# Attention and a gated feed-forward interleaved on one core: where the lead splits w_down, when keys are asked for, and the order of the handover and of the last output groups

## The chip, the cores and the metric

The kernel runs on one core of a Trainium2 chip. The metric is the device time of one execution in microseconds (us). Three runs of the kernel before took 2699.92 to 2701.48, with a median of 2700.95. One more execution was profiled; its own time was 2699.41, and its span from the first to the last instruction 2697.6.

## The reference

The input x is 2048 tokens of 576 numbers, all in 32-bit floats. There are 32 heads of 18, and the feed-forward is 4608 wide.

```python
def _A_ref(x, wqkv, wo):
    qkv = (x @ wqkv).reshape(B, S, 3, H, Dh).transpose(2, 0, 3, 1, 4)
    scores = jnp.einsum("bhqd,bhkd->bhqk", q, k) * (Dh ** -0.5)
    o = jnp.einsum("bhqk,bhkd->bhqd", _softmax(scores), v)
    return o.transpose(0, 2, 1, 3).reshape(B, S, D) @ wo

def _B_ref(x, w_gate, w_up, w_down):
    return (_gelu(x @ w_gate) * (x @ w_up)) @ w_down

xn = _layernorm(x)
return x + _A_ref(xn, ...) * _silu(_B_ref(xn, ...))
```

## The kernel before

**Numbers as two parts.** TensorE multiplies a reduced format. Each operand is therefore split into a high part and the rest (`hi`, `lo`), and each product is three matmuls: high with high, low with high, high with low. A split is two instructions: a copy that rounds (hi), and a subtraction (lo). `split` (L90) puts both on POOL. `split_av` (L95) puts the copy on ACT and the subtraction on DVE.

**Stages.** A prologue normalises x, projects queries, keys and values, and leaves them in DRAM. After it everything is cut into 144 sections of the feed-forward, made by `section` (L394). One section is a block of 512 tokens with 128 of the 4608 columns: 54 matmuls for gate (`pg`) and up (`pu`), then the gelu (`activate`, L357: t1 and t2 by turns on ACT and DVE). `finish` (L426) splits the section's result into `hh` and `hl`. Two sections share one piece of w_down (256 rows). Each odd section asks for it (`raw`), and its `finish` splits it into `dh` and `dl`. `downs` (L422) then runs the down projection of the pair, half after each of the next two sections: 24 matmuls into `py`, each group of six added to Y by DVE. The weights of the next section are asked for and split (`wh`, `wl`, always on POOL) while the present one runs.

- **Lead**: sections 0 to 8. Beside the feed-forward they hold the first score maxima. `FIRST` says how many slots each has (0, 3, 5, 5, 5, 5, 5, 6, 6); a slot is two matmuls `pm` and two maxima `mx` on DVE. Keys are loaded in chunks of eight slots by `load_k`, 12 DMAs each; a loop after each section decides which chunk to ask for (L702). `finish()` uses `split`, so hh, hl, dh and dl are on POOL.
- **Attention**: sections 9 to 136, by a loop over `n` from 0 to 127, with exponentials `pT` (ACT), values `acc` and maxima for a later unit.
- **Tail**: sections 137 to 143, `n` from 128 to 134, in the loop at L743. Here `finish` uses `split_av`. The attention's output of the last 512 tokens is loaded to `OT` (`load_o`, with `den` the reciprocal sums), multiplied (`norm_o`), split on POOL (`split_o`: `oh`, `ol`) and projected by `project_o`: eight groups of 15 matmuls `po`, each copied to `S2` by ACT. The groups are handed out by `at(n, part, ...)`: groups 0 to 3 in sections 138 to 141, groups 4 and 5 in 142, groups 6 and 7 in 143. After the last `downs` (48 matmuls) come, for each of the eight output pieces: tanh on ACT (L354), two DVE operations (L355, L762), the addition of x on POOL (L763) and a store.

**What sets the order.** Instructions of TensorE stand in the order written. A scheduler orders the other engines' instructions, but for those under `keep_in_program_order`. Every DMA goes through the one queue of SP, in order: a DMA that waits holds back those behind it. Each engine works its own queue in order too.

**Buffers.** The tag `raw` has two tiles in the pool `wts` (L99). Weights of gate and up and the raw w_down take turns in them; in sections 139 and later w_down has its own in the pool `epi`. `pT` has four tiles in the pool `att` and is first used by section 9. `wh` and `wl` have five, `hh` and `hl` three, `dh` and `dl` one until the tail and two there, t1 and t2 one, `oh` and `ol` one. In PSUM, `py` has two and `pm` and `po` three.

Of the kernel before, what the change touches and what calls it, by code (L numbers as in the profile page):

```python
# [8 lines left out]
F32 = mybir.dt.float32  # L9
# [57 lines left out]
def kernel(ctx: ExitStack, tc: tile.TileContext, x, wqkv, wo, w_gate, w_up, w_down, out):  # L67
# [22 lines left out]
    def split(hi, lo, raw):  # L90
        first = nc.gpsimd.tensor_scalar(hi, raw, 1.0, 1.0, op0=ALU.mult, op1=ALU.mult)  # L91
        nc.gpsimd.tensor_tensor(lo, raw, f(hi), op=ALU.subtract)  # L92
        return first

    def split_av(hi, lo, raw, keep=lambda i: i):  # L95
        keep(nc.scalar.activation(hi, raw, AF.Copy))  # L96
# [329 lines left out]
    def finish(pool=ffn, cut=split, bufs=1):  # L426

        n = FF["n"] - 1
        b, r = divmod(n // G, NR)
        hh = ffn.tile([P, TB], F32R, name="hh", bufs=G + 1)  # L430
        hl = ffn.tile([P, TB], F32R, name="hl", bufs=G + 1)
        cut(hh, hl, FF["act"])
        FF["hs"].append((hh, hl))
        if n % G == G - 1:
            wd = [pool.tile([P, G, D], F32R, name=m, bufs=bufs) for m in ("dh", "dl")]
            cut(*wd, FF["rawd"])
            for h in range(2):
                FF["down"].append((b, r, FF["hs"], wd, FF["Y"], (2 * h, 2 * h + 1), n + 1 + h))

# [29 lines left out]
    def split_o(i):  # L469

        j = i % (TB // P)
        oh, ol = (op.tile([KO, NK, P], F32R, name=m) for m in ("oh", "ol"))
        split(oh, ol, OT[:, :, j * P:(j + 1) * P])
        OG["o"] = oh, ol

# [14 lines left out]
        rows, cc = place(b, i)  # L490
        nc.sync.dma_start(out[rows, cc], OG.pop(("y", b, i)))

    def project_o(b, i, S2=None):
# [5 lines left out]
        o = OG["o"]  # L499
        terms = [(k, x, w) for k in range(NK) for x, w in ((0, 0), (0, 1), (1, 0))]  # L500
        for m, (k, x, w) in enumerate(terms):
            n = min(KO, D - k * KO)
            nc.tensor.matmul(po[:, 0:288], o[x][0:n, k, :], OW[w][0:n, k, :], start=(m == 0), stop=(m == len(terms) - 1))  # L503
        if b < NB - 1:
            nc.vector.scalar_tensor_tensor(yy, yy, 0.5, po[:, 0:288], op0=ALU.mult, op1=ALU.mult)
            nc.gpsimd.tensor_tensor(yy, yy, xx, op=ALU.add)
            OG["y", b, i] = yy
        else:
            nc.scalar.activation(S2[:, j, cc], po[:, 0:288], AF.Copy)

# [15 lines left out]
    for b in range(NB):  # L526
        last = b == NB - 1
        for k in range(NK):
            t0 = b * AB + max(-(-min(H, (k + 1) * HO) // QD) * NA + 3, 2 * NA + 10 + 3 * k)
            if not (last and k == NK - 1):  # L530
                at(t0, 0, load_o, b, k)
                at(t0 + 2 - last, 2, norm_o, k)
        first = (b + 1) * AB + 1 if last else max((b + 1) * AB + 6, (b + 1) * NR * G - len(FIRST) + 3)
        at(first - 2, 0, load_wo, 0)
        at(first - 1, 2, split_o, 0)
        for i in range(GROUPS):
            n = first + i
            past = i - (ENDS - 2 - first) if last else -1
            if past >= 0:
                n = ENDS - 2 + past // 2  # L540
            if not last:
                at(n, 0, load_xy, b, i)
                at(n + 1, 0, store_y, b, i)
            part = 3 if past >= 0 and past % 2 else 1
            at(n, part, lambda b=b, i=i: project_o(b, i, S2[0]))
            if i == TB // P - 1:
                at(n + 1, 0, load_wo, 1)
            if i + 1 < GROUPS:
                at(n, part + 1, split_o, i + 1)


    with tc.tile_pool(name="att", bufs=1, reuse_waits="tile") as att:
# [138 lines left out]
        def reciprocals(u, rt):  # L691
            den = DEN.pop(u)
            tc.keep_in_program_order(nc.vector.reciprocal(den, den))
            nc.sync.dma_start(rt.rearrange("a (c s) -> a c s", s=QD * TB // P), den)

        load_k(0)
        load_q(0)
        slot, chunk = 0, 1
        for n, m in enumerate(FIRST):
            section([lambda s=s: lead_pair(s) for s in range(slot, slot + m)], "s" if n == 1 else "f")  # L700
            slot += m
            while chunk < KB and chunk * SLOTS <= slot + 14:  # L702
                load_k(chunk, tc.keep_in_program_order)
                chunk += 1
            if n == 3:
# [31 lines left out]
    with tc.tile_pool(name="epi", bufs=1, reuse_waits="tile") as epi:  # L737
        S2[0] = epi.tile([P, TB // P, D], F32, name="S2")
        XX = epi.tile([P, TB // P, D], F32, name="XX")
        n = NU * NA  # L740
        load_o(NB - 1, NK - 1, epi)
        todo[n, 2].insert(0, lambda: norm_o(NK - 1))
        while FF["n"] < NF:  # L743
            section([], "m" if n % 2 else "f", wts if n < NU * NA + 2 else epi)
# [5 lines left out]
            for part in (2, 3, 4):  # L750
                tasks(n, part)
            finish(epi, lambda *t: split_av(*t, tc.keep_in_program_order), 2)
            n += 1
        assert not todo
        downs()
        for Y, j, c in finals:
            cc = slice(288 * c, 288 * c + 288)
            rows = slice(S - TB + j * P, S - TB + (j + 1) * P)
# [3 lines left out]
            nc.vector.scalar_tensor_tensor(ss, th, 0.5, ss, op0=ALU.mult, op1=ALU.mult)  # L762
            nc.gpsimd.tensor_tensor(ss, ss, XX[:, j, cc], op=ALU.add)  # L763
            nc.sync.dma_start(out[rows, cc], ss)


# [26 lines left out]
```

## Time and profile before

| what | us |
|---|---|
| median of three runs | 2700.95 |
| the profiled execution, its own time | 2699.41 |
| its span | 2697.6 |
| PE busy in it | 2654.8 |
| lead, first matmul of section 0 to the first of section 9 | 199.7 to 309.4 |
| attention, to the first matmul of section 137 | 309.4 to 2580.7 |
| tail | 2580.7 to 2697.6 |

The profile's views used below: a table of stretches gives for each its length and the busy time of each engine (and in brackets the number of instructions), then the clock that TensorE was granted as a share of full speed, and the DMA share and rate. The timeline gives an instruction's start, its duration, what it is (out<-in), and in square brackets how long the engine had been idle before it and which instruction or DMA ended that. The chain of waits gives the work that ended last, step by step. Some matmul records are missing, so counts can fall short by a few.

### The profile page before, as it was taken

The page shows a single profiled execution, that of the slowest core. Times are in us where ns is not written, and L with a number is a line of the kernel's source. Part 1 is how long each engine was busy: PE and PEld are TensorE (multiplying, and loading weights), DVE is VectorE, ACT ScalarE, POOL GpSimd, SP SyncE. Part 2 cuts the span into 40 slices and gives each one's busy share as a digit, 9 for nine tenths or more (in the row PEclk, how much of TensorE's full clock was granted, in tenths as well). Part 3 has the DMA queues.
Part 4 walks back from the last instruction along what each step waited for, and adds up shares of the span by engine and source line. Part 5 has one row for each costly group of instructions (what it writes and reads, how often), then busy time and mean ns, then how long its engine had stood idle before and what let it go on. Part 6 is the DMA issues. An engine that isn't in the chain of part 4 may idle for free.

```text
span 2697.6 us, 55502 instructions
## 1 busy us (share of the span) xinstructions
PE 2654.8 (98%) x21000; PEld 2041.0 (76%) x21000; DVE 2005.5 (74%) x3430; ACT 1430.2 (53%) x2542; POOL 1363.9 (51%) x1454
## 2 busy tenths in 40 slices
PE   8998999999999999999999999999999999999997
PEld 7887777777777777777777777777777777777676
DVE  6326888888888877788888877888888877888344
ACT  3221355556665555566656554566555555665622
POOL 2116644444465555545456555454456555444563
PEclk9999999999999999999999999999999999999999
DMA  8874433333354334533345344433435445333341
GB/s 256 262 235 125 111 95 102 104 104 103 101 141 116 102 102 119 137 104 103 103 111 147 102 115 128 130 102 99 103 98 138 118 121 140 104 100 87 75 117 39
DMA packets 389144, 323.65 MB, mean 120 GB/s; under 512 B 105544, under 2 KB 302664, under 8 KB 388876
## 3 DMA queue, kind: packets, MB, share of 16 engines
q1 hardware_dynamic: 388876, 320.08, 43.9%
q8 instruction: 167, 2.74, 0.4%
q14 instruction: 101, 0.83, 0.1%
HBM read 266.58 MB, written 52.85 MB: 118 GB/s over the span
## 4 chain that ended last, share of the span: by engine, by line
PE 94%; DVE 3%; POOL 2%; DMA 1%; ACT 1%; issue 0%; SPq 0%; POOLq 0%; DVEq 0%
PE pg L347 27%; PE acc L666 17%; PE py L377 17%; PE pe L632 10%; PE pm L605 9%; PE po L152 7%; PE pu L347 6%; PE po L503 2%; PE pt L206 0%; DMA raw<-in_B_w_up_dram 0%; DVE Y L355 0%; POOL wl L92 0%; DVE mx L606 0%; DVE Y L383 0%; POOL dl L92 0%
## 5 line engine op out<-in xcount | busy, mean ns | idle before, releaser
L633 ACT ACTIVATE pT<-pe 128x512 f32<-128x512 f32 x2048 | 1164.6, 598 | 770.5 <-PE pm L605 551.8
L606 DVE TENSOR_REDUCE mx<-pm 128x1 f32<-128x512 f32 x2048 | 1291.4, 685 | 57.6 <-PE pm L605 35.2
L347 PE MATMUL pg<-xd,wh 64*128 64x512 f32 x2592 | 949.9, 399 | 7.6 <-POOL wh L91 7.6
L347 PE MATMUL pu<-xd,wh 64*128 64x512 f32 x2592 | 950.5, 399 | 0.1
L632 PE MATMUL pe<-q,KS 56*128 56x512 f32 x2048 | 815.3, 406 | 0.1
L605 PE MATMUL pm<-KS,q 54*128 54x512 f32 x2048 | 798.0, 394 | 3.5 <-DVE mx L606 3.0
L91 POOL TENSOR_SCALAR wh<-raw 128x384 fp32r<-128x384 f32 x432 | 221.7, 514 | 888.0 <-DMA raw<-in_B_w_up_dram 505.3
L347 PEld LDWEIGHTS pg<-xd,wh 64*128 64x128 f32 x2592 | 484.5, 187 | 63.5 <-issue 21.1
L347 PE MATMUL pg<-xd,wl 64*128 64x512 f32 x1296 | 510.4, 394 | 1.3 <-POOL wl L92 1.3
L347 PE MATMUL pu<-xd,wl 64*128 64x512 f32 x1296 | 509.0, 393 | 0.0
L347 PEld LDWEIGHTS pu<-xd,wh 64*128 64x128 f32 x2592 | 485.8, 187 | 6.7 <-DVE t L364 1.3
L666 PE MATMUL acc<-pT,VS 128*32 128x512 f32 x4096 | 466.0, 595 | 0.0
L92 POOL TENSOR_TENSOR wl<-raw,wh 128x384 fp32r<-128x384 f32 x432 | 438.1, 1015 | 34.2
L632 PEld LDWEIGHTS pe<-q,KS 56*128 56x128 f32 x2048 | 369.0, 184 | 81.0 <-ACT pT L633 23.0
L383 DVE TENSOR_TENSOR Y<-py,Y 128x288 f32<-128x288 f32 x544 | 248.0, 457 | 207.4 <-PE py L377 206.7
L605 PEld LDWEIGHTS pm<-KS,q 54*128 54x128 f32 x2048 | 376.9, 185 | 33.1 <-DVE mx L606 7.5
L377 PE MATMUL py<-dh,hh 128*128 128x288 f32 x1152 | 358.0, 311 | 4.7 <-ACT dh L96 2.1
L377 PE MATMUL py<-dl,hh 128*128 128x288 f32 x1152 | 340.5, 296 | 3.7 <-POOL dl L92 2.7
L377 PE MATMUL py<-dh,hl 128*128 128x288 f32 x1152 | 339.0, 294 | 0.4 <-POOL hl L92 0.4
L666 PEld LDWEIGHTS acc<-pT,VS 128*32 128x32 f32 x4096 | 120.1, 109 | 276.6 <-issue 265.2
L377 PEld LDWEIGHTS py<-dh,hh 128*128 128x128 f32 x1152 | 216.6, 188 | 82.8 <-issue 44.6
L347 PEld LDWEIGHTS pg<-xd,wl 64*128 64x128 f32 x1296 | 243.1, 188 | 21.4 <-POOL wl L92 2.3
(104 smaller groups left out, 2816.1 us busy)
## 6 DMA issues: line engine op xcount, KB each, us to landing
KS<-qk SPq DMA_DIRECT2D x1536, 36.0 KB
raw<-in_B_w_gate_dram SPq DMA_DIRECT2D x144, 288.0 KB
raw<-in_B_w_up_dram SPq DMA_DIRECT2D x144, 288.0 KB
raw<-in_B_w_down_dram SPq DMA_DIRECT2D x72, 576.0 KB
VS<-vs SPq DMA_DIRECT2D x128, 152.0 KB
qk<-t SPq DMA_DIRECT2D x72, 256.0 KB
q<-qk SPq DMA_DIRECT2D x384, 36.0 KB
xd<-xhs SPq DMA_DIRECT2D x24, 384.0 KB
```

The costliest lines, as they stand in the source:

```text
L91: first = nc.gpsimd.tensor_scalar(hi, raw, 1.0, 1.0, op0=ALU.mult, op1=ALU.mult)
L92: nc.gpsimd.tensor_tensor(lo, raw, f(hi), op=ALU.subtract)
L152: nc.tensor.matmul(o, st, m, start=(i == 0), stop=(i == len(TERMS) - 1))
L347: nc.tensor.matmul(o, w[1 + wp][k][rr, c, :], xd[xp][k][rr, c, :], start=(i == 0), stop=(i == len(terms) - 1))
L377: nc.tensor.matmul(py, a[:, tt], w[:, g, cc], start=(n == 0), stop=(n == 3 * G - 1))
L383: nc.vector.tensor_tensor(yy, py, yy, op=ALU.add)
L503: nc.tensor.matmul(po[:, 0:288], o[x][0:n, k, :], OW[w][0:n, k, :], start=(m == 0), stop=(m == len(terms) - 1))
L605: nc.tensor.matmul(pm, QS[u, r][rr, t * P:(t + 1) * P], KS[(u * NA + c) % KB][r][rr, :], start=True, stop=True)
L606: nc.vector.tensor_reduce(MX[u][:, 2 * r + a, t, c:c + 1], pm, axis=AX.X, op=ALU.max)
L632: nc.tensor.matmul(pe, KS[(u * NA + c) % KB][r][rr, t * P:(t + 1) * P], QS[u, r][rr, :], start=True, stop=True)
L633: nc.scalar.activation(PT[u, kt][:, 2 * r + a, :], pe, AF.Exp, scale=SCALE)
L666: nc.tensor.matmul(ACC[u][32 * a:32 * a + 32, :], VS[(u * NA + c) % VB][:, v:v + 32], pt[:, a, :], start=(kt == 0), stop=(kt == NT - 1), s ...
```

## The change

Six edits are made.

1. In the lead, the raw w_down goes to a tile of `pT` in place of a `raw` tile (`lead_raw`).
2. In the lead, `finish` uses the new `split_ap`: the copies `hh` and `dh` on ACT, the subtractions `hl` and `dl` on POOL.
3. The test for the next chunk of keys has 11 in place of 14, so chunks 2, 4, 5 and 6 are asked for one section later.
4. At the handover, the last `load_o` stands after section 137's requests in place of before them, and the section whose DMAs and weight requests keep program order is 138 in place of 137 (`keep` in `section`). The scheduler then puts section 138's gate, up and w_down requests on SP before the store of the last `acc`.
5. In section 143 the last w_down is split early (`early`), at the start of the section.
6. Group 5 of `project_o` goes from section 142 to after section 143's `downs`; groups 6 and 7 go behind the last 48 matmuls. Their `oh` and `ol` are split ahead, group 7's into tiles of its own. These two groups aren't copied to S2: DVE multiplies the gate with `po` straight from PSUM, and DVE adds x. The other six pieces end as before.

```diff
+    def split_ap(hi, lo, raw):
+        nc.scalar.activation(hi, raw, AF.Copy)
+        nc.gpsimd.tensor_tensor(lo, raw, f(hi), op=ALU.subtract)
...
-    def section(specials=(), tag="f", pool=wts):
+    def section(specials=(), tag="f", raw_d=None, early=None):
...
-        keep = tc.keep_in_program_order if n == NU * NA + len(FIRST) else lambda i: i
+        keep = tc.keep_in_program_order if n == NU * NA + len(FIRST) + 1 else lambda i: i
...
-            raw = FF["rawd"] = raw_tile([P, G, D], pool)
+            raw = FF["rawd"] = raw_d() if raw_d else raw_tile([P, G, D])
             nc.sync.dma_start(raw, w_down[r * G * P:(r + 1) * G * P, :].rearrange("(g p) n -> p g n", p=P))
+            if early:
+                FF["wd"] = early(raw)
...
-            wd = [pool.tile([P, G, D], F32R, name=m, bufs=bufs) for m in ("dh", "dl")]
-            cut(*wd, FF["rawd"])
+            wd = FF.pop("wd", None)
+            if not wd:
+                wd = [pool.tile([P, G, D], F32R, name=m, bufs=bufs) for m in ("dh", "dl")]
+                cut(*wd, FF["rawd"])
...
+            if last and n >= ENDS - 1:
+                continue
...
-            part = 3 if past >= 0 and past % 2 else 1
-            at(n, part, lambda b=b, i=i: project_o(b, i, S2[0]))
+            at(n, 1, lambda b=b, i=i: project_o(b, i, S2[0]))
...
+        def lead_raw():
+            t = att.tile([P, QD, TB], F32, name="pT", bufs=4)
+            return t.rearrange("p a t -> p (a t)")[:, 0:G * D].rearrange("p (g d) -> p g d", g=G)
...
-            section([lambda s=s: lead_pair(s) for s in range(slot, slot + m)], "s" if n == 1 else "f")
+            section([lambda s=s: lead_pair(s) for s in range(slot, slot + m)], "s" if n == 1 else "f", lead_raw)
             slot += m
-            while chunk < KB and chunk * SLOTS <= slot + 14:
+            while chunk < KB and chunk * SLOTS <= slot + 11:
...
-            finish()
+            finish(cut=split_ap)
...
-        load_o(NB - 1, NK - 1, epi)
...
+            if n == NU * NA:
+                load_o(NB - 1, NK - 1, epi)
...
+        HIND = ENDS - 1 - (NU * NA + 1)
+        project_o(NB - 1, HIND, S2[0])
+        os = []
+        for i in range(HIND + 1, GROUPS):
+            split_o(i, op if i == HIND + 1 else epi)
+            os.append(OG.pop("o"))
         downs()
...
+            if c * (TB // P) + j > HIND:
+                late[c * (TB // P) + j] = th, ss, j, cc
+            else:
+                nc.vector.scalar_tensor_tensor(ss, th, 0.5, ss, op0=ALU.mult, op1=ALU.mult)
+                put(ss, j, cc, nc.gpsimd)
+        for i, o in zip(range(HIND + 1, GROUPS), os):
+            th, ss, j, cc = late[i]
+            po = project_o(NB - 1, i, o=o)
+            nc.vector.scalar_tensor_tensor(ss, th, 0.5, po, op0=ALU.mult, op1=ALU.mult)
+            put(ss, j, cc, nc.vector)
```

The number of matmuls is the same. In the attention's sections the order of instructions on every engine is the same as before.

More of the change, by code (lines that the diff above doesn't have):

```diff
@@ L467, in load_wo, with split_o @@
             nc.sync.dma_start(f(w)[0:D - m, NK - 1, :], wos[i, m:D, cc])
-    def split_o(i):
+    def split_o(i, pool=op):
         j = i % (TB // P)
-        oh, ol = (op.tile([KO, NK, P], F32R, name=m) for m in ("oh", "ol"))
+        oh, ol = (pool.tile([KO, NK, P], F32R, name=m) for m in ("oh", "ol"))
         split(oh, ol, OT[:, :, j * P:(j + 1) * P])
@@ L507, in project_o @@
             OG["y", b, i] = yy
-        else:
+        elif S2 is not None:
             nc.scalar.activation(S2[:, j, cc], po[:, 0:288], AF.Copy)
+        return po[:, 0:288]
     AB = NQ * NA
@@ L537 @@
             n = first + i
-            past = i - (ENDS - 2 - first) if last else -1
-            if past >= 0:
-                n = ENDS - 2 + past // 2
+            if last and n >= ENDS - 1:
+                continue
             if not last:
@@ L548 @@
             if i + 1 < GROUPS:
-                at(n, part + 1, split_o, i + 1)
+                at(n, 2, split_o, i + 1)
     with tc.tile_pool(name="att", bufs=1, reuse_waits="tile") as att:
@@ L740, with cut, early @@
         n = NU * NA
-        load_o(NB - 1, NK - 1, epi)
         todo[n, 2].insert(0, lambda: norm_o(NK - 1))
+        def cut(hi, lo, raw):
+            split_av(hi, lo, raw, tc.keep_in_program_order)
+        def early(raw):
+            wd = [epi.tile([P, G, D], F32R, name=m, bufs=2) for m in ("dh", "dl")]
+            cut(*wd, raw)
+            return wd
         while FF["n"] < NF:
-            section([], "m" if n % 2 else "f", wts if n < NU * NA + 2 else epi)
+            section([], "m" if n % 2 else "f", (lambda: raw_tile([P, G, D], epi)) if n > NU * NA + 1 else None,
+                    early if n == ENDS - 1 else None)
+            if n == NU * NA:
+                load_o(NB - 1, NK - 1, epi)
             if n == NU * NA + 3:
@@ L749, with put @@
             downs()
-            for part in (2, 3, 4):
-                tasks(n, part)
-            finish(epi, lambda *t: split_av(*t, tc.keep_in_program_order), 2)
+            tasks(n, 2)
+            finish(epi, cut, 2)
             n += 1
         assert not todo
-        downs()
+        HIND = ENDS - 1 - (NU * NA + 1)
[4 more added lines that the diff above has]
+            os.append(OG.pop("o"))
+        downs()
+        def put(ss, j, cc, add):
+            rows = slice(S - TB + j * P, S - TB + (j + 1) * P)
+            add.tensor_tensor(ss, ss, XX[:, j, cc], op=ALU.add)
+            nc.sync.dma_start(out[rows, cc], ss)
+        late = {}
         for Y, j, c in finals:
             cc = slice(288 * c, 288 * c + 288)
-            rows = slice(S - TB + j * P, S - TB + (j + 1) * P)
             th = epi.tile([P, 288], F32, name="thl", bufs=len(finals))
```

7 lines of the change are left out of this document (2 added, 5 removed).

## The prediction

> **What bounds the kernel now.** I read the page first, with the chain of waits.
>
> ```profile
> PE 2654.8 (98%) x21000; PEld 2041.0 (76%) x21000; DVE 2005.5 (74%) x3430; ACT 1430.2 (53%) x2542; POOL 1363.9 (51%) x1454
> PE 94%; DVE 3%; POOL 2%; DMA 1%; ACT 1%; issue 0%; SPq 0%; POOLq 0%; DVEq 0%
> ```
>
> TensorE (PE) sets the end nearly everywhere. The change takes no matmul away, so it can only win time in which PE stands, runs at a lower clock, or has finished. The chain names POOL, DMA and DVE for a few per cent, so I asked for stretches cut at the first `pg` matmul of each section. The lead from the end of section 2 on: its `py` work with the wait behind it, then one section a row from section 3 (section 4 is left out; its `py` part stands alone below), and two attention sections:
>
> ```profile
> 223.83:231.49 7.66, 3.73 (x26) 3.29 (x25) 4.39 (x9) 1.18 (x2) 3.65 (x5) 0.98 0.40 98
> 231.49:246.56 15.07, 14.14 (x89) 11.12 (x89) 9.12 (x16) 1.23 (x2) 8.19 (x11) 0.79 0.32 99
> ...
> 258.34:270.12 11.78, 11.66 (x90) 9.38 (x89) 9.85 (x18) 1.23 (x2) 6.30 (x8) 1.00 0.57 147
> 270.12:283.81 13.69, 12.18 (x89) 9.46 (x89) 9.93 (x18) 1.23 (x2) 10.07 (x10) 1.00 0.35 81
> 283.81:296.54 12.73, 12.49 (x94) 9.87 (x93) 11.61 (x23) 1.23 (x2) 6.39 (x8) 1.00 0.59 155
> 296.54:309.44 12.90, 11.64 (x92) 10.38 (x91) 10.47 (x19) 1.23 (x2) 10.06 (x10) 1.00 0.52 143
> 309.44:327.28 17.84, 17.77 (x144) 13.69 (x143) 14.24 (x24) 10.18 (x18) 8.88 (x12) 1.00 0.39 102
> 327.28:344.60 17.32, 17.32 (x143) 12.75 (x142) 14.00 (x23) 10.22 (x18) 11.72 (x13) 1.00 0.39 103
> ```
>
> ```profile
> 254.57:258.34 3.77, 3.65 (x26) 3.25 (x25) 3.64 (x8) 1.18 (x2) 2.16 (x3) 1.00 0.45 82
> ```
>
> An undisturbed lead section of five slots takes 11.78 with PE busy for 11.66. Section 3 takes 15.07, at a mean clock of 0.79, and section 6 takes 13.69. What they wait for stands in the timelines of PE, POOL, ACT and SP:
>
> ```profile
> 231.49 0.79 PE L347 MATMUL pg<-xd,wh 64*128 64x512 f32 x1 [3.02 <-POOL wh L91]
> ```
>
> ```profile
> 222.44 2.64 POOL L92 TENSOR_TENSOR dl<-raw,dh 128x1152 fp32r<-128x1152 f32 x1
> 229.00 0.62 POOL L91 TENSOR_SCALAR hh<-t 128x512 fp32r<-128x512 f32 x1 [3.92 <-DVE t L364]
> ...
> 246.72 1.15 POOL L91 TENSOR_SCALAR dh<-raw 128x1152 fp32r<-128x1152 f32 x1 [6.87 <-PE py L377]
> ...
> 271.50 0.51 POOL L91 TENSOR_SCALAR wh<-raw 128x384 fp32r<-128x384 f32 x1 [6.24 <-DMA raw<-in_B_w_up_dram]
> ```
>
> ```profile
> 215.24 0.60 ACT L360 ACTIVATE t<-pg 128x512 f32<-128x512 f32 x1 [6.58 <-POOL hl L92]
> ```
>
> ```profile
> 214.49 5.69 SPq L573 DMA_DIRECT2D KS<-qk  x12
> 220.28 0.62 SPq L106 DMA_DIRECT2D raw<-in_B_w_gate_dram  x1
> ```
>
> POOL is half idle, but in order: section 3's `wh` stands behind the `hh` at 229.00, which waits for DVE. Later it starves too: the weights at 271.50 are late, because w_down takes turns with them in the two `raw` tiles. The tail, cut the same way (section 143 with parts of its own):
>
> ```profile
> 2590.83:2594.86 4.03, 0.00 (x1) 0.00 (x0) 1.73 (x3) 0.89 (x2) 3.86 (x5) 0.79 1.07 304
> 2594.86:2609.92 15.06, 14.25 (x94) 11.91 (x94) 4.95 (x7) 3.18 (x5) 9.53 (x12) 0.83 0.52 126
> 2609.92:2622.08 12.16, 11.98 (x94) 10.43 (x93) 5.13 (x8) 2.07 (x4) 11.58 (x14) 1.00 0.66 195
> ...
> 2646.41:2660.55 14.14, 13.96 (x109) 12.41 (x108) 6.13 (x10) 2.91 (x5) 3.88 (x4) 1.00 0.14 50
> 2660.55:2676.82 16.27, 14.02 (x110) 12.47 (x109) 6.38 (x10) 4.55 (x8) 4.57 (x4) 1.00 0.00 1
> ...
> 2687.52:2697.60 10.08, 0.00 (x0) 0.00 (x0) 5.55 (x11) 0.44 (x1) 4.53 (x5) 0.56 0.25 89
> ```
>
> ```profile
> 2660.55:2666.94 6.39, 6.39 (x56) 5.30 (x55) 1.95 (x1) 0.93 (x2) 2.29 (x2) 1.00 0.00 0
> 2666.94:2669.02 2.08, 2.08 (x18) 2.08 (x17) 0.70 (x2) 1.23 (x2) 0.00 (x0) 1.00 0.00 0
> ...
> 2674.75:2676.82 2.07, 0.00 (x1) 0.01 (x1) 0.72 (x2) 1.98 (x3) 0.00 (x0) 1.00 0.00 0
> 2676.82:2678.21 1.39, 0.39 (x1) 0.18 (x1) 1.34 (x1) 0.00 (x0) 0.00 (x0) 1.00 0.00 0
> 2678.21:2682.10 3.89, 3.89 (x18) 3.89 (x18) 1.28 (x3) 0.89 (x2) 0.00 (x0) 0.56 0.00 0
> ```
>
> PE stands 4.03 at the handover, then works section 138 off at clock 0.83, in 15.06 where the next takes 12.16. Ahead of the last 48 matmuls it stands 2.07 and 1.00, then runs at 0.56. After them come 10.08 in which PE does nothing.
>
> **The lead, edits 1 to 3.** Nine copies `hh` and four `dh` go from POOL to ACT. The tail has them on ACT already:
>
> ```profile
> 2675.09 0.62 ACT L96 ACTIVATE hh<-t 128x512 fp32r<-128x512 f32 x1
> 2675.61 1.15 ACT L96 ACTIVATE dh<-raw 128x1152 fp32r<-128x1152 f32 x1
> ```
>
> The durations are those of POOL (0.62 at 229.00, 1.15 at 246.72), and ACT has room (1.23 busy of 11.78). POOL keeps `hl` and `dl`. In order of time:
>
> - `hl` of section 0 no longer waits for `hh` on POOL, and ACT's next gelu (215.24) waited for that `hl`. Through DVE's order that sets section 2's end: 0.62, with the gap between the two 0.7.
> - Section 2's `py` waited for `dl`. With `hh` and `dh` on ACT beside it, `dl` (2.64 from 222.44) ends about 1.9 earlier (0.62 + 1.15 + gaps). In the new order section 3's weights follow it on POOL, with no `hh` between, and their DMA goes out before chunk 2 of the keys, at 214.5 and not 220.28. So 7.66 falls to the plain 3.77: 3.9.
> - Without the gap the clock stays up: section 3 falls from 15.07 to 11.78: 3.3.
> - Section 6 starved through the shared tiles. Now `raw` serves gate and up alone, two sections ahead, so 13.69 falls to 11.78: 1.9.
> - Sections 7 and 8 have six slots and a late `dl`. I take 12.2 for each (11.78 and one slot) against 12.73 and 12.90: 1.2.
>
> Sum 11.0. What is late next: `dh` has one tile, and must wait until `py` of the pair before has read it (246.72 shows that wait on POOL). Now it stands on ACT, with the next `hh` queued behind it, and with that `hl`, and the next gelu that reuses t1. After that `py` ends, `dh`, `dl` and `hl` take 1.15 + 2.64 + about 1.3 (half of `dl`) = 5.1 one after the other, and the next gelu comes 8.0 later (11.78 less 3.77), so I price it at 0. If the cover is gone, each such pair loses up to 1.9, the loss of section 6. The keys: 12 DMAs a chunk hold SP for 5.69, now behind a request for weights. Chunk 2 would go out from 216 to 221.5; its first slot (16) is in section 4, near 239. Chunk 6 stands before the eight DMAs with the maxima of unit 0, which the first score needs; by SP's order these still land about 4 ahead of section 9. DVE has 9.85 of work in 11.78 and isn't the next bound. Bounds: 5 (only half of the stalls go, nothing from section 6 on) to 12.5 (`py` without waits).
>
> **The handover, edit 4.** Timeline of POOL, and the chain of waits:
>
> ```profile
> 2590.32 1.27 POOL L459 TENSOR_TENSOR OT<-OT,den 72x512 f32<-72x512 f32 x1 [10.05 <-DMA den<-rT]
> 2591.68 0.72 POOL L91 TENSOR_SCALAR oh<-OT 126x640 fp32r<-126x640 f32 x1
> 2592.49 1.84 POOL L92 TENSOR_TENSOR ol<-OT,oh 126x640 fp32r<-126x640 f32 x1
> ```
>
> ```profile
> 2587.70 5.50 DMA raw<-in_B_w_up_dram
> ```
>
> ```profile
> 2568.20 2.69 POOL L92 TENSOR_TENSOR dl<-raw,dh 128x1152 fp32r<-128x1152 f32 x1
> ```
>
> Section 138's weights wait twice: on SP behind `den`, and on POOL behind `OT`, `oh` and `ol`, where POOL idles 10.05. Their tile is free when this last `dl` ends, at 2570.9. In the new order they are asked for then, land by 2578 (5.50 and the issues), and all three splits stand ahead of `OT`. So PE goes on at 2590.83: 4.03, and with the clock up 15.06 becomes 12.16: 2.9 more. Sum 6.9. The moved requests pass, on SP, `den` of the heads before, the store of `acc`, the loads of `OT` and the last `den`. The store and what follows it wait for work that ends after 2577, so they lose nothing. The earlier `den` goes out some 3 later, and with it POOL's first multiplication and `hl` of section 136; that is needed only by section 137's gelu, at 2587. Group 0 needs `ol`, now behind two `oh` (its own and group 7's): 2590.32 + 1.27 + 2 x 0.72 + 1.84 = 2594.9, and PE gets to it at 2597.2 (2590.83 + 6.39). Bounds: 3 (a stall stays and the clock falls) to 7.5.
>
> **The last groups, edits 5 and 6.** Section 142 loses group 5: 14.14 to 12.16, 2.0. In section 143 group 6 (2.08) and the wait of 2.07 go, as the early `dh` and `dl` are ready and `hh` and `hl` are covered by `py` and group 5: 16.27 to 12.1, 4.15. The wait for `dl` (1.0) goes, and the stretch of 3.89 at clock 0.56 shrinks by 3.89 x 0.44 = 1.7: 2.7. From the eighth `py` on, DVE has the same eight gates to work off. Two multiply-and-add pairs end there instead of with POOL; groups 6 and 7 (2 x 2.08 of PE) hide behind the six other gates. I take 10.08 unchanged. Sum of the two edits 2.0 + 6.85 = 8.85, bounds 4 and 11.
>
> By the Trainium skill (TensorE: Matmul & The Clock Gate, What's actually happening), idleness of about 3.4 us halves the clock until some 3.4 us of work have passed. By that, as an estimate, each of three cold stretches gives 1.7 back, 5.1 in all, where the rows give 3.3, 2.9 and 1.7; the sum would be 24. That rows show a drop already after 3.02 and after 2.07 and 1.00 speaks for the rows.
>
> **Sum.** 11.0 + 6.9 + 2.0 + 6.85 = 26.7, from the profiled execution's 2699.4: 2672.7. That one lies 1.5 under the median of the runs, so I say 2674.
>
> **Rivals.**
>
> 1. *ACT's queue becomes the lead's wait* (`dh` behind `py`, `hh` behind `dh`). For it: 6.87 of that wait at 246.72. Against: POOL bore it in a section of 11.78. The lead then gives 5: 2680. Chance 0.14.
> 2. *The handover's stall only moves* to `OT`, `oh`, `oh`, `ol`, or the request isn't early in fact, so that edit doesn't do what it says. For it: `den` lands 2590. Against: 2 of margin. 2678 to 2681. Chance 0.09.
> 3. *The end becomes DVE's.* Operations on DVE beside POOL's additions stretch:
>
> ```profile
> 2687.97 0.36 DVE S L762
> ...
> 2690.40 1.93 DVE thl L355 x2
> ```
>
>    Two take 1.93, with POOL's additions running; one of the same size takes 0.36 at 2687.97, before they overlap. DVE gets two additions more, at the very end. With four operations so stretched (4 x 0.6) and the groups' `po` waiting for the slowed `py`, the last part gives 4.5 and not 8.85: 2678. Against: POOL has two additions less. Chance 0.12. The Trainium skill (SBUF — State Buffer, SBUF: two separate sides) says that DVE with two inputs from SBUF and POOL shut each other out for a whole instruction; the row agrees, and by the rule the two additions on DVE themselves no longer collide.
> 4. *The attention slows.* Starting 11 earlier and with other requests before it, SP could ask for weights later against each section. POOL waits for them already:
>
> ```profile
> POOL wh L91 <- DMA raw<-in_B_w_up_dram: 505.3, 103, 26.2
> ```
>
>    If the 127 later sections took 17.84 like the first and not 17.32, the loss is 66: 2740. It decides from 26.7 / 127 = 0.21 a section. Against: these sections' order is unchanged on all engines, and the lead takes four tiles from the ring of four `pT` and four fewer from the ring of two `raw`, so each buffer stands as before. Chance 0.07.
>
> **How the numbers follow.** My forecast has 0.58: alone 2668 to 2680, by half the way to the terms' bounds. Rivals 1 to 3, singly or two together, reach 2686. With all terms at their upper bounds it is 2668.3 by 12.5 + 7.5 + 11, with the 1.5 added 2670; I go to 2666 for sections that lose more than I see. Range 2666 to 2686; above lie rival 4 and misses of all three parts. Some 0.2% (5.4) can be told from no change in this kernel. Rival 4 gives 0.05 for slower, and in a mild form 0.02 for no change; the rest is faster, 0.93.
>
> **What would show it.** Right: in the lead, sections of 11.8 and 12.2 from section 3 on, none with a clock under 1.00, section 9 starting near 298.5; PE without a gap at the handover, section 138 in 12.2; the last `py` starting about 12.1 after section 143 does; the end some 10 after the eighth `py`. Wrong: `py` or `pg` waiting for POOL or ACT in the lead, a first `po` that waits for `ol`, DVE operations over 0.8 after the last `po`, or attention sections over 17.4.

## The result, and the profile after

The changed kernel takes 2673.61 us (median of four runs, 2672.62 to 2675.06), beside 2701.11 for the kernel before in the same comparison. The ratio is 0.99, its 95% interval 0.9887 to 0.9913. The forecast was 2674. Measured once more, beside the experiments, it took 2672.07 against 2698.23, a ratio of 0.9904 (0.9886 to 0.9921).

The profiled execution took 2674.07, with a span of 2672.3. Its page, busy time and chain of waits:

```profile
PE 2648.8 (99%) x21000; PEld 2025.0 (76%) x21000; DVE 2007.3 (75%) x3432; ACT 1440.9 (54%) x2553; POOL 1354.0 (51%) x1439
PE 96%; DVE 2%; DMA 0%; ACT 0%; issue 0%; POOL 0%; SPq 0%; DVEq 0%
```

PE's share of the chain rises from 94 to 96%; POOL and DMA no longer have one. The stretches, cut as before: sections 0 to 2 without the last `py` work, that `py` work, section 3, sections 6, 7 and 8, then sections 138, 142 and 143 (the last without its final matmuls), and the stretch from the second addition of the last `downs` to Y up to the end:

```profile
199.79:224.38 24.59, 21.82 (x179) 17.98 (x179) 13.01 (x21) 6.11 (x9) 19.17 (x23) 1.00 0.61 156
224.38:228.14 3.76, 3.64 (x25) 3.24 (x25) 3.64 (x8) 1.19 (x2) 3.68 (x6) 1.00 0.67 168
228.14:239.92 11.78, 11.66 (x89) 9.38 (x88) 9.86 (x18) 1.86 (x3) 6.38 (x8) 1.00 0.50 138
...
263.47:275.24 11.77, 11.65 (x89) 9.37 (x89) 9.85 (x18) 2.92 (x4) 8.38 (x8) 1.00 0.41 97
275.24:288.02 12.78, 12.54 (x94) 9.67 (x94) 11.62 (x23) 2.23 (x4) 5.87 (x7) 1.00 0.59 140
288.02:299.90 11.88, 11.65 (x92) 10.44 (x91) 10.59 (x19) 2.56 (x4) 8.44 (x8) 1.00 0.54 166
...
2582.10:2594.27 12.17, 11.99 (x96) 10.44 (x95) 6.89 (x10) 3.97 (x6) 11.91 (x13) 1.00 0.64 165
2630.76:2642.93 12.17, 11.97 (x94) 10.31 (x94) 5.67 (x9) 4.60 (x7) 3.88 (x4) 1.00 0.16 57
2642.93:2654.81 11.88, 11.88 (x95) 10.51 (x94) 6.53 (x11) 1.86 (x3) 0.00 (x0) 1.00 0.00 1
...
2656.60:2672.30 15.70, 9.64 (x66) 8.63 (x65) 12.44 (x25) 3.27 (x8) 6.04 (x7) 0.93 0.22 77
```

Set beside the rows of before: every section of the lead from 3 to 6 takes 11.76 to 11.78 at full clock, there is no gap at the handover, section 138 takes 12.17 and not 15.06, and sections 142 and 143 have lost what the prediction took off. At the handover POOL now splits section 138's first weights (`wh`) ahead of the multiplication to `OT` for the last heads, and not behind it:

```profile
2571.02 0.52 POOL L91 TENSOR_SCALAR wh<-raw 128x384 fp32r<-128x384 f32 x1 [0.79 <-DMA raw<-in_B_w_up_dram]
...
2581.69 1.29 POOL L467 TENSOR_TENSOR OT<-OT,den 72x512 f32<-72x512 f32 x1 [3.95 <-DMA den<-rT]
```

By stage, from the two profiled executions (us):

| stage | before | after | won | forecast |
|---|---|---|---|---|
| lead, section 0 to the start of 9 | 109.76 | 100.11 | 9.65 | 11.0 |
| attention, to the start of 137 | 2271.27 | 2272.19 | -0.92 | 0 |
| sections 137 and 138, with the gap | 29.21 | 22.18 | 7.03 | 6.9 |
| sections 139 to 142 | 50.63 | 48.66 | 1.97 | 2.0 |
| 143 to the second of the last eight additions to Y | 20.51 | 13.67 | 6.84 | 6.85 |
| from there to the end | 16.5 | 15.7 | 0.8 | 0 |

The wins add up to 25.4; the start of section 0, 0.11 later, makes the 25.3 between the two spans. The stages will be used below in place of whole times wherever they can be: differences of one or two us in the whole time drown in the attention, as the control shows next.

### The profile page after: what moved, and what is told of

Same layout as the page of the kernel before. It is cut to its first block, busy times and chain, and to the rows that moved or that the text cites. A ratio compares the mean times of both kernels' runs of the same rounds, so it can differ in the third digit from the quotient of the medians.

```text
span 2672.3 us, 55506 instructions
## 1 busy us (share of the span) xinstructions
PE 2648.8 (99%) x21000; PEld 2025.0 (76%) x21000; DVE 2007.3 (75%) x3432; ACT 1440.9 (54%) x2553; POOL 1354.0 (51%) x1439
## 4 chain that ended last, share of the span: by engine, by line
PE 96%; DVE 2%; DMA 0%; ACT 0%; issue 0%; POOL 0%; SPq 0%; DVEq 0%
PE pg L351 27%; PE acc L673 17%; PE py L381 17%; PE pe L639 10%; PE pm L612 9%; PE pu L351 7%; PE po L156 7%; PE po L511 2%; DVE mx L613 1%; PE pt L210 0%; DVE Y L387 0%; DVE t L365 0%; DVE Y L359 0%; PE pm L622 0%; DMA xx<-in_A_x_dram 0%
```

## The experiments

Twelve kernels ran, in three groups of four with the kernel before beside them (2698.2 to 2698.9 in all three). The first below is the changed kernel itself; the others have one or more of its edits undone, or something added.

### The control, and the attention's length

> The changed kernel once more, as a control beside the kernels that undo one edit. My theory: 2673.6 within 2, attention (first matmul of section 9 to that of section 137) 2272.2 as in its first profile, so that the 2268.3 to 2270.6 of the kernels that undo parts come from these parts. Rival (the length of the attention differs from execution to execution): an attention of 2268 to 2271 here too, with the code unchanged.

It took 2672.07. Stretches of the attention as a whole, first in the first profile of the changed kernel, then in this one:

```profile
299.90:2572.09 2272.19, 2271.30 (x18521) 1700.53 (x18520) 1796.88 (x3037) 1338.42 (x2361) 1188.62 (x1258) 1.00 0.42 110
```

```profile
298.71:2569.31 2270.60, 2269.57 (x18519) 1707.15 (x18519) 1793.89 (x3037) 1335.89 (x2361) 1187.86 (x1258) 1.00 0.41 110
```

Identical code, 1.6 apart. Over all kernels here, whose attention is written the same, it ran from 2267.6 to 2272.2. The rival of this expectation holds: the attention's length differs by execution, by 1.6 here with the code unchanged, and the 0.92 lost in the first profile need not be the change's. So rival 4 of the prediction is false, and a whole time here can't settle less than about 2 us.

### The lead: all three edits undone

```diff
-            section([...], "s" if n == 1 else "f", lead_raw)
+            section([...], "s" if n == 1 else "f")
...
-            while chunk < KB and chunk * SLOTS <= slot + 11:
+            while chunk < KB and chunk * SLOTS <= slot + 14:
...
-            finish(cut=split_ap)
+            finish()
```

> The changed kernel with edits 1 to 3 undone (the lead as before). My theory (edits are independent, and each is worth the loss of its own stage): the lead goes back to about 309.4 - 199.7 and the end of it to some 9.5 to 11 later, so 2683 to 2685 against 2673.6; section 3 takes 15.1 again at a clock near 0.79, and section 6 13.7. Rival (what the lead gives is taken back later, because the attention's requests start from another state): the loss at the lead is the same, but the time changes by under 7, the rest comes back between section 9 and section 137.

It took 2682.53, but its runs lie from 2677.5 to 2686.95. In the profiled one (span 2685.2) section 3 takes 15.49 at clock 0.78 and section 6 13.32, near the 15.1 and 13.7 expected. Its section 8 takes 17.38, where the kernel before took 12.90, though the order of instructions up to there is the same on POOL, ACT, DVE and SP. PE's longest wait in it:

```profile
308.85 0.61 PE L381 MATMUL py<-dl,hh 128*128 128x288 f32 x1 [3.20 <-POOL dl L92]
```

In the kernel before this wait was 1.26, and the clock stayed at 1.00; here the section's mean clock is 0.80. `dl` is late because POOL's queue begins late: its first `wh` of the section starts 2.8 after the section does, where it started 0.8 after. The view names a `pm` for this, but by the trace 14 of the 16 parts of the `w_up` load that this `wh` reads had landed by 297.96, and the last two at 299.14 and 299.91; `wh` started at 300.08. In the kernel before, `wh` started 0.18 after its load's last part. So the late end of one DMA cost some 4.5 in this execution. The profiled run is the slowest of the five, but how often this happens no second profile shows. What the lead gives is kept to the end: the attention took 2270.55. So the rival falls.

### The lead: one edit undone at a time

The three lines of the diff above, each undone alone:

> The changed kernel with edit 1 alone undone (w_down of the lead in the raw tiles again). My theory: section 6 starves as before, 13.3 to 13.7 in place of 11.78, the rest of the lead unchanged: +1.9. Rival (w_down's tile also holds up the weights of section 3): section 3 takes 15 again and section 2's end a wait of 3, +5 or more.

> The changed kernel with edit 2 alone undone (hh and dh of the lead on POOL again). My theory: the terms 0.7 and 3.9 at the end of section 2 come back, +4.6, and with a gap of 3 before section 3 also 3.3 of a lower clock, +7.9 at most; sections 4 to 6 stay at 11.8, section 8 gets up to 1 longer. Rival (the earlier weights of edits 1 and 3 cured section 2 and 3): under +2.

> The changed kernel with edit 3 alone undone (14 again, chunk 2 of the keys ahead of section 3's weights on SP). My theory: section 3's weights are asked for 5.7 later and land about 226, in time for the 228 at which it starts: 0 to +1. Rival (the keys ahead of the weights made the gap of 3.02): section 3 waits 2 or more for its weights and runs at a lower clock, +3 to +6.

The times: 2672.05, 2672.68 and 2676.95 against the control's 2672.07. w_down in the shared tiles (edit 1 undone) costs nothing, and section 6 doesn't starve. Its row, and then sections 0 to 2 and section 3 with the copies on POOL again, and the same two with the keys early again:

```profile
261.11:272.88 11.77, 11.65 (x89) 9.37 (x88) 9.84 (x18) 2.92 (x4) 9.05 (x10) 1.00 0.49 138
```

```profile
199.96:229.88 29.92, 25.47 (x202) 22.34 (x203) 16.54 (x28) 4.97 (x7) 24.88 (x30) 1.00 0.61 163
229.88:241.80 11.92, 11.73 (x89) 9.46 (x89) 10.00 (x18) 1.23 (x2) 7.35 (x10) 1.00 0.42 130
```

```profile
200.12:230.77 30.65, 25.55 (x202) 21.45 (x202) 17.20 (x29) 8.03 (x11) 20.75 (x25) 1.00 0.61 168
230.77:246.37 15.60, 14.36 (x88) 11.35 (x89) 9.12 (x16) 1.23 (x2) 8.20 (x11) 0.78 0.46 125
```

The control took 27.34 and 11.78 for these two. With the copies on POOL the first stretch is 2.6 longer. Of this, 1.2 is a longer wait for q at the start of section 1, which differs between executions with this part of the code unchanged. The other 1.4 is edit 2's: PE waits 1.56 and not 0.97 for the maxima (`mx`) in section 2, which stand behind the gelu that needs section 0's `hl`, and 0.91 for `dl`, where the control doesn't wait. Section 3 keeps its clock. With the keys early, both the gap of 2.83 and the slow section 3 are back: 3.3 and 3.8. My theories for edits 1 and 2 (1.9 and 4.6 to 7.9) were too high, and that for edit 3 (0 to 1) was wrong. Why edit 3 counts so much is in POOL's timeline. First the control, then the kernel with the keys early:

```profile
220.55 2.67 POOL L97 TENSOR_TENSOR dl<-pT,dh 128x1152 fp32r<-128x1152 f32 x1
223.20 0.98 POOL L91 TENSOR_SCALAR wh<-raw 128x384 fp32r<-128x384 f32 x2
...
228.11 1.29 POOL L97 TENSOR_TENSOR hl<-t,hh 128x512 fp32r<-128x512 f32 x1 [0.41 <-DMA raw<-in_B_w_up_dram]
```

```profile
221.48 2.67 POOL L97 TENSOR_TENSOR dl<-pT,dh 128x1152 fp32r<-128x1152 f32 x1
228.98 1.26 POOL L97 TENSOR_TENSOR hl<-t,hh 128x512 fp32r<-128x512 f32 x1 [4.82 <-ACT hh L96]
230.21 0.99 POOL L91 TENSOR_SCALAR wh<-raw 128x384 fp32r<-128x384 f32 x2
```

In the control the weights of section 3 (`wh`) are split straight after `dl`, at 223.20, and `hl` of section 2 comes after them. With the keys ahead of the weights on SP, the scheduler turned this round: `wh` stands behind `hl`. `hl` waits for ACT's `hh`, and that for section 2's gelu, so POOL idles 4.82 with section 3's weights behind it. PE, which has done section 2's `py` by 227.94, waits until 230.77 and then works at the lower clock. The two loads had landed by 227.2 in this trace, so the load itself isn't what PE waited for. The cost is the place of a split in POOL's queue, and edit 3 decides that place. My reckoning for the weights' landing wasn't the point.

### The lead: edits 1 and 2 undone together

> The changed kernel with edits 1 and 2 undone together and edit 3 kept. Undone alone each cost 0 to 0.6, edit 3 undone alone 4.9, all three together some 10. Theory A (edits 1 and 2 stand in for each other, and together carry what edit 3 does not): about +5, 2677, with section 6 at 13.3 or a wait of 3 in section 8. Theory B (edit 3 alone ends the stalls, and the rest of the 10 came from edit 3 meeting the others): 2672 to 2674, sections 3 to 6 at 11.8 and section 8 under 12.5.

It took 2676.92, near 5 more than the control: theory A. Its rows for sections 3 and 8, and POOL's timeline in section 8:

```profile
228.90:240.82 11.92, 11.73 (x89) 9.37 (x89) 9.99 (x18) 1.23 (x2) 7.36 (x10) 1.00 0.45 137
...
288.92:307.49 18.57, 14.24 (x91) 12.79 (x90) 11.16 (x19) 1.23 (x2) 10.46 (x11) 0.82 0.48 113
```

```profile
292.92 0.51 POOL L91 TENSOR_SCALAR wh<-raw 128x384 fp32r<-128x384 f32 x1 [9.49 <-PE pm L612]
...
298.99 2.63 POOL L92 TENSOR_TENSOR dl<-raw,dh 128x1152 fp32r<-128x1152 f32 x1
```

Section 3 is cured by edit 3 alone, section 8 isn't: it takes 18.57 against 11.84. Its `py` waits for `dh` and for `dl`, and the work behind that runs at a lower clock:

```profile
297.87 0.40 PE L381 MATMUL py<-dh,hh 128*128 128x288 f32 x1 [0.93 <-POOL dh L91]
301.68 0.61 PE L381 MATMUL py<-dl,hh 128*128 128x288 f32 x1 [3.41 <-POOL dl L92]
```

Two pairs of `wh` and `wl`, then `hh`, `dh`, `hl` and `dl` stand one after the other on POOL, after 9.49 of idling (here too the view names a `pm`, and the last part of the `w_up` load landed 0.18 before `wh` started), and `dl` ends 12.7 after the section began. With edit 1 undone alone it ends 8.1 after, and with edit 2 undone alone 5.3 after, and neither makes PE wait. So edits 1 and 2 stand in for each other in section 8: one of them is needed, and there it is worth 6.7 of this profile, and 4.9 of the median in all. Section 6, where I had looked for edit 1, takes 11.78 here too.

### The handover

```diff
-        keep = ... if n == NU * NA + len(FIRST) + 1 else lambda i: i
+        keep = ... if n == NU * NA + len(FIRST) else lambda i: i
...
+        load_o(NB - 1, NK - 1, epi)
         todo[n, 2].insert(0, lambda: norm_o(NK - 1))
...
-            if n == NU * NA:
-                load_o(NB - 1, NK - 1, epi)
```

> The changed kernel with edit 4 undone (load_o and program order as before). My theory: +6.9 (2680.5), as a gap of 4.0 before section 138 and 2.9 of a lower clock in it. Rival (the gap came from the whole tail's order and edits 5 and 6 also moved it): under +4, with a shorter gap or no low clock.

It took 2680.96, with runs from 2680.07 to 2684.59. The gap and section 138, then POOL's timeline:

```profile
2580.78:2588.44 7.66, 0.01 (x1) 0.00 (x0) 3.05 (x4) 1.79 (x2) 7.57 (x7) 0.67 0.85 257
2588.44:2603.53 15.09, 14.26 (x95) 11.58 (x95) 3.25 (x6) 2.27 (x4) 9.51 (x13) 0.83 0.39 80
```

```profile
2580.73 1.26 POOL L467 TENSOR_TENSOR OT<-OT,den 72x512 f32<-72x512 f32 x1 [10.47 <-DMA den<-rT]
2582.08 1.73 POOL L91 TENSOR_SCALAR oh<-OT 126x640 fp32r<-126x640 f32 x2
2583.78 3.02 POOL L92 TENSOR_TENSOR ol<-OT,oh 126x640 fp32r<-126x640 f32 x2
2586.78 2.09 POOL L91 TENSOR_SCALAR wh<-raw 128x384 fp32r<-128x384 f32 x2
```

By the medians that is 8.9 above the control and 7.35 above the first comparison, near the 6.9 of my theory. In the profiled execution, which took 2683.35, the stage costs 10.7 more than with the edit (32.85 against 22.18). The gap is 7.66 where it was 4.03 in the kernel before, 3.6 longer. Two `oh` and two `ol` now stand ahead of `wh`, because edit 6 splits group 7's pair here too: the way from `OT` to `wh` is 6.05 and was 3.98, which is 2.1 of it. Another 1.1 is the two `wh` themselves, 2.09 beside DVE's `dl` where they took 0.98 in the kernel before; the rest is `OT` starting later against PE's last work. So edit 6 without edit 4 makes the handover longer than it was in the kernel before (29.21). Section 138 is as cold as in the kernel before, 15.09.

Then the same with 18 matmuls on PE in the gap:

```diff
+            if n == NU * NA:
+                warm = ps.tile([P, TB], F32, name="acc", tag="acc", bufs=1)
+                t = FF["xd"][0][0][:, 0, :]
+                for i in range(18):
+                    nc.tensor.matmul(warm, t[:, 0:P], t, start=(i == 0), stop=(i == 17))
```

> Edit 4 undone as in u_hand, and 18 matmuls that nothing reads added (128x128 by 128x512, into the free tile of the tag acc) after section 137's own work and before section 138, so that PE has some 3.8 of work in the gap of 4.0. My theory (the lower clock of section 138 is the price of the idle PE alone): section 138 runs at 1.00 in 12.2, so +4.0 to +4.6 against the changed kernel (2677.6 to 2678.2), 2.5 to 3 less than u_hand. Rival (section 138 is long because its later weights are late too, and the low clock is only its mean over waits): section 138 keeps some 15 and the time is that of u_hand within 1.

It took 2680.93, the same as without, and this can't be read as the rival's win: the gap was 7.66 and not the 4.0 for which the 18 were meant. The stretch that holds them, and section 138:

```profile
2579.08:2585.73 6.65, 4.18 (x21) 3.11 (x19) 1.92 (x4) 1.79 (x2) 6.56 (x7) 0.97 1.00 298
2585.73:2602.00 16.27, 14.34 (x93) 11.68 (x93) 4.40 (x7) 2.27 (x4) 10.50 (x13) 0.80 0.36 75
```

PE still stood 2.47, worked 0.8, and stood 1.74 more. By the trace the clock fell at 2585.34, still within the wait of 2.47; hence the 0.97 of the first row. The section ran at 0.80. So the trial didn't tell the two theories apart; a cleaner one was made at the end of the kernel.

### The end

```diff
-                    early if n == ENDS - 1 else None)
+                    None)
...
-            if last and n >= ENDS - 1:
-                continue
+            past = i - (ENDS - 2 - first) if last else -1
+            if past >= 0:
+                n = ENDS - 2 + past // 2
...
-            tasks(n, 2)
+            for part in (2, 3, 4):
+                tasks(n, part)
...
-        HIND = ENDS - 1 - (NU * NA + 1)
-        project_o(NB - 1, HIND, S2[0])
...
+        HIND, os = GROUPS, []
```

> The changed kernel with edits 5 and 6 undone (w_down of section 143 split at its end, groups 5 to 7 in sections 142 and 143 as before). My theory: +8.9 by the terms 2.0 + 4.15 + 2.7 (2682.5), with the two idle stretches of PE before the last 48 matmuls back. Rival (part of it is the order at the end that comes after the eighth addition to Y): up to +9.7, the end after that addition 0.6 longer than in the changed kernel.

It took 2678.92. By stages: section 142 14.14, section 143 to the second addition 20.49, from there to the end 16.63; against the control's 12.2, 13.71 and 15.70 that is 1.9 + 6.8 + 0.9 = 9.6, so the end after the additions does give something, as the rival said. In the nine profiles that leave the end as it is, that last stretch takes 15.4 to 15.7, so 16.6 lies outside their spread. The whole time is only 6.85 above the control's; in the profiled execution the attention took 2268.3 and the lead 98.6, together 2.7 less than the control's.

The same kernel with nine matmuls in the first wait before the last 48:

```diff
         HIND, os = GROUPS, []
+        warm = ps.tile([P, TB], F32, name="acc", tag="acc", bufs=1)
+        t = FF["xd"][0][0][:, 0, :]
+        for i in range(9):
+            nc.tensor.matmul(warm, t[:, 0:P], t, start=(i == 0), stop=(i == 8))
```

> Edits 5 and 6 undone as in u_end, and 9 matmuls that nothing reads (128x128 by 128x512, some 2.1 together) put on PE in the wait of 2.07 ahead of the last 48 matmuls. My theory (idle PE alone lowers the clock): the wait of 1.00 stays, the 18 matmuls behind it run in about 2.3 at 1.00 and not 3.94 at 0.57; 1.6 less than u_end. Rival (the clock falls for another reason, or the wait of 1.00 is enough): the same 3.9 and the same time as u_end.

The wait for `dl`, and the matmuls behind it, without and with the nine:

```profile
2655.86:2657.26 1.40, 0.40 (x2) 0.19 (x2) 1.34 (x1) 0.00 (x0) 0.00 (x0) 1.00 0.00 0
2657.26:2661.20 3.94, 3.94 (x18) 3.94 (x19) 1.28 (x3) 0.89 (x2) 0.00 (x0) 0.57 0.00 0
```

```profile
2657.34:2658.73 1.39, 0.39 (x1) 0.18 (x2) 1.34 (x1) 0.00 (x0) 0.00 (x0) 1.00 0.00 0
2658.73:2661.10 2.37, 2.37 (x17) 2.37 (x18) 1.05 (x3) 0.55 (x2) 0.00 (x0) 1.00 0.00 0
```

The wait of 1.0 for `dl` stays, and the matmuls behind it run at 1.00: 2.37 and not 3.94. From the start of section 143 to the end it is 35.6 against 37.1, 1.5 less. So the lower clock is the price of PE standing, and filling the wait with work that nobody reads takes that price away. The whole time, 2678.32, is 0.6 below that of the kernel without them, inside the spread; the stage tells it.

Edit 5 alone undone:

> The changed kernel with edit 5 alone undone (the last w_down split after section 143's gelu). My theory: the waits for dh and dl stand again in front of py, but group 5 now covers none of them before dh is ready: PE stands 2 and 1 and runs at a lower clock for 4, so +3 to +4.7. Rival (w_down needs no early split once the groups are behind the py, because the eight gates of DVE set the end): under +1.

It took 2671.38, no more than the control of another group. By stages it isn't free: from section 143 to the second addition it takes 15.82, 2.1 more than the control, and the end after it 0.2 less, within its spread. Lead and attention, which were together 0.8 shorter in this profile, hide that. The cost is under the 3 to 4.7 that I expected, because group 5 covers the wait for `dh`, and PE stands once, for 1.49. The wait, and the stretch behind it:

```profile
2653.05 0.40 PE L381 MATMUL py<-dl,hh 128*128 128x288 f32 x1 [1.49 <-DVE dl L101]
```

```profile
2653.05:2655.42 2.37, 2.37 (x17) 2.37 (x18) 1.06 (x3) 0.56 (x2) 1.36 (x1) 1.00 0.00 0
```

No lower clock follows it. Edit 5 is worth about 2.1 of the 6.8 beside edit 6. By subtraction edit 6 gives the rest; it wasn't undone alone.

### Two additions

```diff
-        load_k(0)
-        load_q(0)
+        load_q(0)
+        load_k(0)
...
-                put(ss, j, cc, nc.gpsimd)
+                put(ss, j, cc, nc.vector)
```

> The changed kernel with two additions of mine: q of unit 0 asked for before the first keys, and all eight final additions of x on DVE, none on POOL. My theory: the waits for q at the start of section 1 (0.58 to 1.9) go, 0.5 to 1.3 less in sections 0 to 2, as long as the first keys are then not as late; at the end no DVE operation takes over 0.6, which gives back 1.0 to 1.5, less the six additions of 0.45 that DVE does more: 0 to +1.5. Together -1 to +1 against the changed kernel. Rival (POOL's additions stretch no DVE operation, their length has another cause): DVE operations of 0.8 and more also without them, and the end 2 to 3 longer.

It took 2669.26 (0.989, 0.9873 to 0.9906), the shortest of all, and a little shorter than the control; but its attention alone is 2.2 shorter than the control's, so this isn't shown to be a better kernel. The first addition only changes what is late, from q to the keys:

```profile
210.21 0.47 PE L612 MATMUL pm<-KS,q 54*128 54x512 f32 x1 [0.78 <-DMA KS<-qk]
```

The second does what it should. From the second addition to Y to the end, first the control, then this kernel:

```profile
2654.00:2669.70 15.70, 9.63 (x66) 8.62 (x65) 12.44 (x25) 3.25 (x8) 6.03 (x7) 0.94 0.22 77
```

```profile
2653.74:2668.80 15.06, 9.21 (x66) 8.56 (x65) 12.09 (x31) 3.26 (x8) 0.79 (x1) 0.97 0.23 80
```

DVE has six instructions more and is busy 0.35 less. Its operations with both inputs in SBUF now take 0.44 to 0.46 each, but for one of 0.73 that runs beside POOL's last `ol`. So the rival (the length has another cause) falls. The stretch is 0.64 shorter than the control's and 0.35 below the shortest with POOL's additions; I had expected 0 to 1.5 longer.

## Why the prediction was right, and where it wasn't

**The whole (2674, measured 2673.61).** That the two lie 0.4 apart is in part luck: the lead gave 1.35 less than forecast and the end 0.8 more, and the attention's length alone differs by up to 4.6 between these executions. The terms are what can be judged.

**The handover (6.9, measured 7.03).** Right in each step: no gap, clock 1.00, section 138 in 12.17, and no wait for `ol` in front of group 0. The clock's 2.9 was read as the price of the idle PE; the trial at the end of the kernel shows that mechanism, the one at the handover itself failed to. That undoing the edit costs 10.7 in the profile was not foreseen: edit 6 lengthens the very queue on POOL that edit 4 moves away.

**The last groups (8.85, measured 8.81).** 1.97 for section 142 and 6.84 up to the second addition to Y, against 2.0 and 6.85. The cold stretch, 1.7 in the prediction, measured 1.57 by itself (3.94 less 2.37).

**The end (0, measured 0.8).** The step that failed is the one that began at the eighth `py`. DVE's chain begins earlier. DVE in the changed kernel (start, duration, what, idle time before it):

```profile
2656.60 0.46 DVE L387 TENSOR_TENSOR Y<-py,Y 128x288 f32<-128x288 f32 x1 [0.34 <-PE py L381]
...
2663.55 1.43 DVE L359 SCALAR_TENSOR_TENSOR thl<-thl,Y 128x288 f32<-128x288 f32 x2
...
2667.47 0.78 DVE L785 TENSOR_TENSOR S<-S,XX 128x288 f32<-128x288 f32 x1
...
2668.65 0.46 DVE L785 TENSOR_TENSOR S<-S,XX 128x288 f32<-128x288 f32 x1
```

From the second addition to Y at 2656.60 to 2669.1 it has no gap of note. So the end is set by when the second `py` is there and by how long DVE works from then on, 12.44 of 15.70; `py` matmuls and groups 6 and 7 run beside it. In the kernel before this was so already, only that PE's slow `py` let DVE wait a little at first. Rival 3 (the end becomes DVE's) was thus half true before and after. Its price wasn't paid: the slow operations beside POOL's additions are there (1.43 for two, 0.78 for one), but with edits 5 and 6 undone POOL's last additions ended 1.4 after DVE's last operation, and now DVE's own come last.

**The lead (11.0, measured 9.65).** The sum came close and its parts did not.

- *Section 3 and the `py` before it* (3.9 and 3.3). Both were won, but the step that gave them to `dh`, `hh` and an earlier `dl` holds for the smaller part. Undoing the copies on ACT brings back the wait for `dl`, 0.91, and no gap before section 3. Undoing the keys brings back the gap of 2.83 and the lower clock: 7.2 of the lead against the control's profile (whose lead, 99.0, is among the shorter ones), and 4.9 of the median. The prediction named the order on POOL and the requests on SP in one breath with `dl`, and priced the keys' edit at nothing by itself.
- *`hl` of section 0* (0.7). Won, and by edit 2: PE's wait for `mx` in section 2 was 1.68 in the kernel before, is 1.12 and 0.97 in the two profiles of the changed kernel, and 1.56 with the copies on POOL.
- *Section 6* (1.9). Won, but no single edit is needed for it: with any one of the three undone, and with edits 1 and 2 undone together, it stays at 11.8. So the shared tiles alone don't starve it; it was slow only with the keys early as well.
- *Sections 7 and 8* (12.2 each). 12.78 and 11.88 came out, 0.26 over in sum. In section 7 DVE is busy for 11.62 of 12.78, with 23 instructions; a row of before had shown the same 11.61, and I took the extra time for `dl`. In section 8 edits 1 and 2 together are worth what neither is alone.
- *Sections 0 to 2*. The first stretch took 24.59 and not the 23.5 it should have: PE waited up to 1.34 for q at the start of section 1. In the profiles with an unchanged lead it varies, and the whole lead with it, from 98.6 to 100.8; 1.1 of the missing 1.35 lies here.

**Rival 1** (ACT's queue becomes the wait). ACT does wait as it said:

```profile
240.03 1.17 ACT L96 ACTIVATE dh<-pT 128x1152 fp32r<-128x1152 f32 x1 [1.66 <-PE py L381]
241.10 0.62 ACT L96 ACTIVATE hh<-t 128x512 fp32r<-128x512 f32 x1
```

`dh` waits 1.66 for `py` with `hh` behind it, and the sections stay at 11.76 to 11.78. The cover of 8.0 before the next gelu held. **Rival 2** is false by the row of section 138. Of the signs of being wrong, one could tell nothing: 56 of the 128 attention sections take over 17.4 in the kernel before and in the changed one (means 17.74 and 17.75); the row of 17.32 was one of the shorter.

What stays open: why the attention differs by a few us between executions, and why two parts of one load landed 2 us behind the others where all three edits of the lead were undone, and with that how often its section 8 takes 17.38.

## What to carry to other kernels

Where one queue feeds the bound engine, ask which instruction stands ahead of the one that is late, and what the scheduler would have put there had the loads been asked for in another order: moving twelve loads of keys ahead of two of weights still let the weights land in time, but it turned round the order on another engine's queue. Edits that each cost next to nothing when undone alone can be worth 5 together, so undo them in pairs before one is dropped as idle. And when whole times scatter by as much as an edit is worth, compare the stage.

## What the runs showed of the hardware

- PE's clock fell to half after it had stood 2.07 and, after one matmul, 1.00 more; within a single wait of 2.47; and in or after waits of 2.83, 3.02, 3.20 and 4.03. After single waits of 1.00, of 1.49 and of 1.83 (section 2 with the lead's three edits undone) it didn't fall. So for a single wait the border lies somewhere between 1.83 and 2.47 in these runs.
- It stayed at half for 6.8 in section 3 and at the handover of the kernel before, and for 3.4 among its last `py`. That goes with the different prices, 3.3 and 2.9 against 1.7. Two of the stretches:

```profile
231.13:237.94 6.81, 5.81 (x26) 4.27 (x28) 1.29 (x2) 0.00 (x0) 6.73 (x10) 0.50 0.20 66
...
2678.48:2681.88 3.40, 3.40 (x16) 3.40 (x16) 1.28 (x3) 0.78 (x2) 0.00 (x0) 0.50 0.00 0
```

- DVE's additions and multiplications of 128x288 with both inputs in SBUF took 0.45 alone and 0.69 to 0.92 where one of POOL's additions ran beside them for at least a part. An addition with one input in PSUM (`Y<-py,Y` at 2658.71 in the changed kernel) took 0.45 beside them too. With all eight additions on DVE, 31 instructions took 12.09 where 25 had taken 12.44.
